# Summing the decay once per token pair in a fused RWKV6 and Hyena kernel, with one exponential, pre-multiplied k and r, chunks turned in twos, and a new order of work

## The chip, the cores and the metric

One core of one Trainium2 chip runs the program. Its engines are PE (matmul), DVE (vector), ACT (scalar), POOL (general purpose) and SP, whose queue here only issues DMA. Data that matmuls produce lies in PSUM, eight banks of 512 fp32 per partition; all other data lies in SBUF. The metric is the device time of one launch in microseconds (us). The kernel before takes 170.6 us, the median of three runs (170.54 to 171.2).

## The reference

```python
for t in range(S):                                   # S = 768, B, H, D = 4, 8, 48
    y[:, :, t] = einsum('bhd,bhde->bhe', r_t, state + outer(u * k_t, v_t))
    state = w_t[..., None] * state + outer(k_t, v_t)  # w_t in 0.8 to 0.95
x = y.transpose(0, 2, 1, 3).reshape(B, S, 384)
x1, x2, x3 = split(x @ w_proj)                        # three times 384 columns
x2 = irfft(rfft(x2, axis=1) * rfft(filter_fft, axis=0))
out = (x1 * x2 * x3) @ w_out
```

The first half is a linear recurrence over 768 steps with a decay per channel; the second is a projection, a long convolution by Fourier transforms, two gates and a projection back. All of it is fp32 outside; matmul operands are bf16 inside.

## The kernel before

**Pairs.** The recurrence runs in 12 pairs (gi, three for each of the four batches), each of two chunks of 128 steps. On a partition lie two neighbouring tokens, the even one (j = 0) and the odd one (j = 1), so a tile of k, r, v or w has 128 partitions and 8 heads x 2 x 48 elements. For each pair `lw`, `lk`, `lr` and `lv` load 384 KB each through SP's queue. `ws` multiplies the odd w by the even one, `ln` (L1245) takes logarithms of both planes, and `cs` (L1258, L1262) sums them over the tokens of a 64-token block by products with triangular matrices (`before`, `upto`, `ident`) into three PSUM banks, with the whole block's sum beside. ACT then takes exponentials: `ek` (L1267, of the negated sums, two banks into SBUF tile xk), `eq` (L1276, two banks in place) and `ph` (L1270). `km` multiplies k by xk (on DVE or POOL, from SBUF), `qm` (L1286) multiplies r by the exponentials in PSUM (DVE). `tk` and `tq` turn the products on PE and `ck`, `cq` copy them out, or, for some pairs, SP turns them by DMA (L1302).

**Within a pair.** `sc` makes scores between k and r (L1400), `mt` masks them (DVE from PSUM, or ACT's copy `ma` first and DVE from SBUF), `kv` and `su` carry the state on (L1361, L1372), `ys`, `yy` and `yi` (L1381, L1422, L1436) add up the output. `rk` is k times r, turned by `rp` and `rt` (or by DMA, L1323) for the term of u: `cp` (L1333) and `cc`, then `vc` on POOL. `xn` copies each chunk out, `yt` and `xT` (L1455, L1461) turn it for the second half.

**Second half.** When a batch's three pairs are done: `p`, `q` (gates, L1631), `xw` (side projection, L1655), `sd`, `f` (forward transform, L1486), `u`, `z` (product with the filter's spectrum), `E` (inverse, L1722), `aE`, `dE`, `yE` (folding and gating), `o` (output projection, L1793) and `so` (store). The last batch is cut finer. Before all this ACT computes the transform's tables from sines, and PE runs `warm` matmuls that only keep it busy.

**What sets the order.** A table, ORDER, lists every operation by name with the engine that does it and, for those that open PSUM banks, the bank. The program issues the operations in that order, so each engine's queue, SP's DMA queue too, has the order of its rows; waits for data and buffers are added automatically. A third word that names a DVE operation makes a POOL instruction wait for that one as well. `D` is DVE, `N` is DVE reading SBUF, `A` ACT, `G` POOL, `P` PE, `S` SP, `-` means that the operation isn't done; `warm 43 3` is 43 half-width warming matmuls.

## Time and profile before

| | |
|---|---|
| median of three runs | 170.6 us |
| the profiled execution | 171.99 us, its span 170.2 us |
| mean granted PE clock | 0.943 |
| PE, DVE, ACT, POOL busy | 140.2, 128.7, 123.3, 75.8 us |
| DMA | 32.07 MB, mean 188 GB/s |

Busy time of PE is modelled and includes the pipeline's overlap, so PE at 82% is not PE at its peak. A group's mean on the page can mix shapes; the view that keeps shapes apart doesn't. The idle time before an instruction is put down to what released it last.

### The profile page before, as it was taken

How to read it: one execution, taken by the hardware profiler on the slowest of the kernel's cores; microseconds unless marked ns; L12 is line 12 of the kernel's file. 1: busy time of each engine (PE TensorE's matmuls, PEld its weight loads, DVE VectorE, ACT ScalarE, POOL GpSimd, SP SyncE). 2: the span in 40 equal slices, each digit the busy share in tenths (PEclk: the TensorE clock that was granted, in tenths of full speed). 3: DMA queues.
4: the chain of work that ended last, by engine and by line, in shares of the span. 5: the costliest groups of instructions: out<-in, count | busy, mean ns of one | idle time of the engine just before them, and what ended most of it. 6: DMA issues, size and time to landing. Idle time of an engine off the chain costs nothing.

```text
span 170.2 us, 5650 instructions
## 1 busy us (share of the span) xinstructions
PE 140.2 (82%) x2371; PEld 90.2 (53%) x2371; DVE 128.7 (76%) x248; ACT 123.3 (72%) x196; POOL 75.8 (45%) x84
## 2 busy tenths in 40 slices
PE   7748877999889584999987789678399999999960
PEld 2326655676566352666544565455255665666520
DVE  6627989769686579399995889786248999999940
ACT  7788986876899585598997598648258586768740
POOL 7995985597459604841008940791030220002300
PEclk9978997899999999699999999999659999999997
DMA  5999979976999999989899999999912201321884
GB/s 130 312 289 293 267 181 276 273 191 89 226 221 234 260 236 252 184 162 258 223 284 174 214 191 191 193 140 174 184 27 46 49 1 62 131 88 56 323 334 119
DMA packets 77834, 32.07 MB, mean 188 GB/s; under 512 B 73841, under 2 KB 76402, under 8 KB 77810
## 3 DMA queue, kind: packets, MB, share of 16 engines
q1 hardware_dynamic: 76210, 30.55, 77.2%
q0 software_dynamic: 1600, 1.18, 4.8%
q8 instruction: 18, 0.29, 0.7%
q14 instruction: 6, 0.05, 0.1%
HBM read 22.41 MB, written 4.72 MB: 159 GB/s over the span
## 4 chain that ended last, share of the span: by engine, by line
PE 34%; DVE 13%; DMA 4%; ACT 2%; issue 2%; SPq 1%; ACTq 0%; DVEq 0%
PE banks L1631 8%; PE banks L1793 7%; PE banks L1486 7%; PE banks L1722 4%; DMA rt<-rk 4%; DVE U L1084 3%; DVE kq L1286 3%; PE banks L1655 2%; DVE mt L1084 2%; PE banks L1258 1%; DVE P L1695 1%; PE banks L1422 1%; DVE sd L1667 1%; DVE S L1372 1%; PE banks L1361 1%
## 5 line engine op out<-in xcount | busy, mean ns | idle before, releaser
L1631 PE MATMUL banks<-xT,wproj 128*128 128x384 bf16 x144 | 28.3, 326 | 2.4 <-DVE kq L1286 1.7
L1084 DVE TENSOR_TENSOR mt<-banks,causal 128x1024 bf16<-128x1024 f32 x15 | 18.1, 1218 | 6.2 <-PE banks L1400 6.2
L1088 ACT ACTIVATE x<-banks 128x768 bf16<-128x768 f32 (+1 forms) x26 | 17.9, 703 | 6.4 <-PE banks L1655 3.5
L1084 POOL TENSOR_TENSOR vc<-vb,cc 128x768 bf16<-128x768 bf16 x10 | 14.7, 1474 | 16.6 <-ACT xn L1088 10.2
L1084 POOL TENSOR_TENSOR kq<-xk,kr 128x768 bf16<-128x768 f32 x8 | 14.5, 1810 | 16.7 <-DVE U L1084 12.2
L1631 PEld LDWEIGHTS <-wproj 128*128 128x128 bf16 x144 | 13.2, 98 | 10.3 <-issue 3.0
L1084 POOL TENSOR_TENSOR g<-g,x 128x768 bf16<-128x768 bf16 (+1 forms) x4 | 5.1, 1284 | 26.0 <-DVE g L1084 17.9
L1267 ACT ACTIVATE xk<-banks 128x768 f32<-128x768 f32 x12 | 9.7, 812 | 7.7 <-PE banks L1262 7.7
L1258 PE MATMUL banks<-lg,before 128*128 128x384 bf16 x25 | 7.3, 374 | 9.5 <-DVE kq L1286 5.8
L1486 PE MATMUL banks<-sd,F 128*128 128x384 bf16 (+1 forms) x96 | 14.5, 340 | 0.0
L1655 PE MATMUL banks<-wproj,xT 128*128 128x384 bf16 x72 | 13.7, 326 | 0.1
L1793 PE MATMUL banks<-wout,y 128*128 128x384 bf16 (+1 forms) x78 | 13.3, 327 | 0.0
L1286 DVE TENSOR_TENSOR kq<-banks,kr 128x768 bf16<-128x768 f32 x12 | 11.4, 951 | 1.6 <-ACT banks L1276 1.5
L1372 DVE TENSOR_TENSOR S<-banks,phi 128x192 bf16<-128x192 f32 x20 | 7.0, 352 | 7.3 <-PE banks L1361 5.8
L1486 PEld LDWEIGHTS <-F 128*128 128x128 bf16 (+1 forms) x120 | 9.0, 112 | 6.3 <-issue 1.4
L1088 ACT ACTIVATE o<-banks 128x768 f32<-128x768 f32 (+1 forms) x12 | 9.0, 760 | 4.1 <-PE banks L1793 3.8
L1084 POOL TENSOR_TENSOR w<-w 128x384 f32<-128x384 f32 x9 | 8.9, 994 | 6.4 <-DVE kq L1084 6.4
L1084 POOL TENSOR_TENSOR rk<-kr 128x768 bf16<-128x768 f32 x6 | 10.9, 1817 | 1.4 <-DMA kr<-in_k_dram 1.4
L1400 PE MATMUL banks<-qk 48*64 48x128 bf16 x384 | 10.2, 221 | 1.3 <-DMA qk<-kq 0.8
L1084 DVE TENSOR_TENSOR U<-X,hh 128x2304 bf16<-128x2304 bf16 (+1 forms) x12 | 11.1, 952 | 0.1
L1088 ACT ACTIVATE X<-banks 128x768 bf16<-128x768 f32 x11 | 8.7, 812 | 3.3 <-PE banks L1486 2.7
L1088 ACT ACTIVATE xn<-banks 128x384 bf16<-128x384 f32 x20 | 9.0, 490 | 2.4 <-PE banks L1436 2.3
(129 smaller groups left out, 351.7 us busy)
## 6 DMA issues: line engine op xcount, KB each, us to landing
w<-in_w_dram SPq DMA_DIRECT2D x12, 384.0 KB, 5.4
v<-in_v_dram SPq DMA_DIRECT2D x12, 384.0 KB, 5.1
kr<-in_k_dram SPq DMA_DIRECT2D x12, 384.0 KB, 5.6
kr<-in_r_dram SPq DMA_DIRECT2D x12, 384.0 KB, 5.2
out_dram<-o SPq DMA_DIRECT2D x11, 384.0 KB, 2.4
U<-in_moe_filter_fft_dram SPq DMA_DIRECT2D x2, 576.0 KB, 6.5
...
```

What stands on the lines that cost most here:

```text
L1084: return eng(e).tensor_mul(o, a, b)
L1088: return nc.scalar.activation(out=o, in_=a, func=AF.Copy)
L1258: nc.tensor.matmul(p[:, z, 0:C], m, x, start=n == 0, stop=n == len(terms) - 1)
L1267: op(f"ek{gi}", [ACT], lambda e, bk: nc.scalar.activation(out=xk[sx].rearrange("p j h d -> p j (h d)"), in_=three(bk, f"cs{gi}")[:, 1:3, 0 ...
L1286: op(f"qm{gi}", [DVE], lambda e, bk: nc.vector.tensor_mul(kqq[:, 1, :, :, 0:D], three(bk, f"cs{gi}")[:, 0:2, 0:C].rearrange("p j (h d) -> ...
L1372: op(f"su{i}", [DVE], lambda e, bk, kvp=kvp, sn=sn, c=c: nc.vector.tensor_mul(stt[sn], kvp(bk), phi[sq][:, :, c:c + 1].to_broadcast([L, HP ...
L1400: nc.tensor.matmul(p[spans[c], par, i, jk, :].rearrange("p (j t) -> p j t", j=2), qkk[x, 0, jk, 2 * a + i, spans[c]], qkk[x, 1, :, 2 * a + ...
L1486: nc.tensor.matmul(p[rows], F[:, ti, c0 + rows.start:c0 + rows.stop], x[q][:, ti, :], start=(ti == 0), stop=(ti == NT - 1),)
L1631: nc.tensor.matmul(o, wproj[:, cb, col0:col0 + L], x, start=(cb == 0), stop=(cb == CB - 1))
L1655: nc.tensor.matmul(view(bk)[:, z], xT[bx][:, cb, (c0 + z) * L:(c0 + z + 1) * L], wproj[:, cb, C:2 * C], start=(cb == 0), stop=(cb == CB - 1),)
L1722: nc.tensor.matmul(o, P[:, q, m, cs], x, start=start, stop=stop)
L1793: nc.tensor.matmul(view(bk)[:, j] if full else view(bk)[spans[j]], y[cb][:, j, p0:p0 + m], wout[:, cb, :], start=(cb == 0), stop=(cb == CB ...
```

## The change

The even and odd decay are no longer summed apart. `ws` writes the product of both w to a tile of its own (wp), `ln` takes its logarithm (384 columns instead of 768), and `cs` makes two sums into two banks: `before` times it, and `upto`, now filled with -1, times it. One exponential `ex` over both banks, in place, serves k and r. To make up for the missing plane, `kw` multiplies the even k by the odd w and `rw` the odd r by the even w, after `rk` has read both; `km` and `qm` then both read PSUM, on DVE. Where the order says `ws -`, as it does for pairs 0 to 4 and 10, the product isn't made and `ln` and `cs` take both planes, with four wide products instead of two. xn holds both chunks of a pair and one `yt` and `xT` turn both, except for pair 11; xT's layout puts a chunk's blocks side by side. `u` and `z` are made in two pieces (of two and one block). Code that loads v in bf16 through POOL's queue and a second form of the inverse's copy are there too; the order uses neither. The flips of the tables (`if`) run on ACT, all six angle pieces (`ia`) on DVE. The whole order is new.

The start, on ACT: rows from the last table load on (lg is the logarithm, xk and `banks<-banks` are exponentials, phi the block's decay). Before:

```order
L1565 ACT_TABLE_LOAD
L1245 ACTIVATE lg_69<-w_61 128x8x2x48
L1245 ACTIVATE lg_70<-w_62 128x8x2x48
L1267 ACTIVATE xk_71<-banks 128x768
L1276 ACTIVATE banks<-banks 128x2x384
L1270 ACTIVATE phi_77<-banks 128x8
L1267 ACTIVATE xk_72<-banks 128x768
L1276 ACTIVATE banks<-banks 128x2x384
```

Now:

```order
L1599 ACT_TABLE_LOAD
L1271 ACTIVATE lg_71<-w_61 128x8x2x48
L1271 ACTIVATE lg_72<-w_62 128x8x2x48
L1293 ACTIVATE banks<-banks 128x2x384
L1104 ACTIVATE vb_85<-v_67 128x768
L1104 ACTIVATE cc_83<-banks 128x16
L1296 ACTIVATE phi_77<-banks 128x8
L1296 ACTIVATE phi_78<-banks 128x8
L1293 ACTIVATE banks<-banks 128x2x384
L1104 ACTIVATE qk_75<-banks 128x1024 x2
```

One exponential per pair stands where two stood, and the copy of v and the turned q and k come sooner.

POOL, early pairs (kq is the product for k, kr the tile of k and r, w the decay). Before:

```order
L1084 TENSOR_TENSOR kq_74<-xk_72,kr_65 128x16x48
L1084 TENSOR_TENSOR rk_80<-kr_65 128x768
L1084 TENSOR_TENSOR rk_79<-kr_66 128x768
L1084 TENSOR_TENSOR vc_88<-vb_85,cc_83 128x768
L1084 TENSOR_TENSOR kq_73<-xk_71,kr_66 128x16x48
L1084 TENSOR_TENSOR w_61<-w_61 128x8x48
```

Now:

```order
L1100 TENSOR_TENSOR rk_79<-kr_66 128x768
L1100 TENSOR_TENSOR kr_66<-kr_66,w_63 128x8x48 x2
L1100 TENSOR_TENSOR vc_88<-vb_85,cc_83 128x768
L1100 TENSOR_TENSOR vc_89<-vb_86,cc_84 128x768
L1100 TENSOR_TENSOR kr_64<-kr_64,w_61 128x8x48
L1105 CAST vb_87<-v_67 128x768
```

The products for k have left POOL; the halves of k and r by w, which need only loads, stand in their place.

The end, on ACT, from the last pair's xn on (x, g, ev, o, X and x_106 or x_104 are what PE made: gate, second gate, inverse, output, transform and side projection). Before:

```order
L1088 ACTIVATE xn_99<-banks 128x2x4x48
L1088 ACTIVATE x_106<-banks 128x768
L1088 ACTIVATE x_102<-banks 128x2x192 x2
L1088 ACTIVATE ev_111<-banks 128x384
L1088 ACTIVATE o_124<-banks 128x768
L1088 ACTIVATE g_103<-banks 128x4x192
L1088 ACTIVATE ev_112<-banks 128x384
```

Now:

```order
L1104 ACTIVATE xn_96<-banks 128x2x4x48 x2
L1104 ACTIVATE x_100<-banks 128x4x192
L1104 ACTIVATE x_104<-banks 128x768
L1104 ACTIVATE x_104<-banks 128x384
L1104 ACTIVATE g_101<-banks 128x2x192
L1776 ACTIVATE ev_110<-banks 128x384
L1104 ACTIVATE o_122<-banks 128x768
```

Pair 11 now runs ahead of pair 10, so the last xn is that of pair 10; behind it stand fewer of batch 2's gates, inverses and outputs than stood behind pair 11.

```diff
--- before.py
+++ after.py
-ek0 A
-km0 D
-cs1 P 4
-eq0 A
...
+ex0 A
+vb0 A
...
+qm0 D
...
+km0 D
...
@@ -1007,8 +1020,8 @@
     wl = tiles(NW, [L, H, 2, D], FP32, "w")
     kr = tiles(NR, [L, 2, H, 2, D], FP32, "kr")
     vl = tiles(NV, [L, H, 2, D], FP32, "v")
+    wp = tiles(NX, [L, H, D], FP32, "wp")
     lg = tiles(NL, [L, 2, H, DP], BF16, "lg")
-    xk = tiles(NX, [L, 2, H, D], FP32, "xk")
     kq = tiles(NK, [L, 2, 2, H, DP], BF16, "kq")
     qk = tiles(NQ, [L, 2, 2, HP, L], BF16, "qk")
     phi = tiles(NQ, [L, HP, 2], FP32, "phi")
@@ -1019,9 +1032,9 @@
     vc = tiles(NVC, [L, H, 2, D], BF16, "vc")
     mt = tiles(NM, [L, 2, 2, 2, 2, L], BF16, "mt")
     stt = tiles(NS, [L, HP, D], BF16, "S")
-    xn = tiles(NXN, [L, C], BF16, "xn")
-
-    xT = tiles(2, [L, CB, S], BF16, "xT")
+    xn = tiles(NXN, [L, 2, C], BF16, "xn")
+
+    xT = tiles(2, [L, NCH, CB, L], BF16, "xT")
     x1 = sb.tile([L, CB, 2, HALF], BF16, name="x1")
     g = tiles(2, [L, CB, 2, HALF], BF16, "g")
     sd = sb.tile([L, 2, NT, C], BF16, name="sd")
...
@@ -1235,58 +1251,66 @@
         load("w", W, w, f"w.{sw}")
         load("k", kr[sr][:, 0], k, f"k.{sr}")
         load("r", kr[sr][:, 1], r, f"r.{sr}")
...
+        def apart(bk):
             return bk[f"how ws{gi}"] == NONE
 
-        op(f"ws{gi}", [POOL, DVE, NONE], lambda e, bk: mul(e, W[:, :, 1], W[:, :, 0], W[:, :, 1]),
-           r=[f"w.{sw}"], w=[f"w.{sw}"], n=C, k="ssf")
-        op(f"ln{gi}", [ACT], lambda e, bk: nc.scalar.activation(
-            out=lgg.rearrange("p j h d -> p h j d")[:, :, :, 0:D], in_=W, func=AF.Ln),
-           r=[f"w.{sw}", "exp", "pads"], w=[f"lg.{sl}"], n=2 * C, k="s")
+        op(f"ws{gi}", [POOL, DVE, NONE], lambda e, bk: mul(e, wp[sx], W[:, :, 0], W[:, :, 1]),
+           r=[f"w.{sw}"], w=[f"wp.{sx}"], n=C, k="ssf")
+
+        def ln(e, bk):
+            if apart(bk):
+                return nc.scalar.activation(
+                    out=lgg.rearrange("p j h d -> p h j d")[:, :, :, 0:D], in_=W, func=AF.Ln)
+            return nc.scalar.activation(out=lgg[:, 0, :, 0:D], in_=wp[sx], func=AF.Ln)
+
+        op(f"ln{gi}", [ACT, ACT2], ln, r=[f"w.{sw}", f"wp.{sx}", "exp", "pads"], w=[f"lg.{sl}"], n=C, k="s", n2=2 * C)
 
         def cs(e, bk):
-            p = three(bk, f"cs{gi}")
-            le, ls = lgg[:, 0, :, 0:D], lgg[:, 1, :, 0:D]
-            if both(bk):
-                sums = (((before, le), (before, ls)), ((upto, le), (before, ls)), ((upto, le), (upto, ls)))
-            else:
-                sums = (((before, ls),), ((before, ls), (ident, le)), ((upto, ls),))
-            for z, terms in enumerate(sums):
-                for n, (m, x) in enumerate(terms):
-                    nc.tensor.matmul(p[:, z, 0:C], m, x, start=n == 0, stop=n == len(terms) - 1)
-            planes = (0, 1) if both(bk) else (1,)
+            p = two(bk, f"cs{gi}")
+            ns = (0, 1) if apart(bk) else (0,)
+            for z, m in enumerate((before, upto)):
+                for n in ns:
+                    nc.tensor.matmul(p[:, z, 0:C], m, lgg[:, n, :, 0:D], start=n == 0, stop=n == ns[-1])
             for hp in range(HP):
-                for n in planes:
-                    nc.tensor.matmul(p[:, 2, C + 2 * hp:C + 2 * hp + 2], lgg[:, n, 2 * hp:2 * hp + 2, :], chunk,
-                                     start=n == planes[0], stop=n == planes[-1])
-
-        op(f"cs{gi}", [PE], cs, r=[f"lg.{sl}", "m.before", "m.ident", "m.chunk", "pads"], new={f"cs{gi}": 3},
-           pe=[("128", C)] * 4 + [("128", 2)] * 4, pe2=[("128", C)] * 6 + [("128", 2)] * 8)
-        op(f"ek{gi}", [ACT], lambda e, bk: nc.scalar.activation(
-            out=xk[sx].rearrange("p j h d -> p j (h d)"), in_=three(bk, f"cs{gi}")[:, 1:3, 0:C], func=AF.Exp, scale=-1.0),
-           r=["exp"], w=[f"xk.{sx}", f"ek.{gi}"], uses=[f"cs{gi}"], n=2 * C, k="p")
+                for n in ns:
+                    nc.tensor.matmul(p[:, 1, C + 2 * hp:C + 2 * hp + 2], lgg[:, n, 2 * hp:2 * hp + 2, :], chunk,
+                                     start=n == 0, stop=n == ns[-1])
+
+        op(f"cs{gi}", [PE], cs, r=[f"lg.{sl}", "m.before", "m.chunk", "pads"], new={f"cs{gi}": 2},
+           pe=[("128", C)] * 2 + [("128", 2)] * 4, pe2=[("128", C)] * 4 + [("128", 2)] * 8)
+
+        def ex(e, bk):
+            p = two(bk, f"cs{gi}")[:, :, 0:C]
+            return nc.scalar.activation(out=p, in_=p, func=AF.Exp)
+
+        op(f"ex{gi}", [ACT], ex, r=["exp"], w=[f"ex.{gi}"], uses=[f"cs{gi}"], n=2 * C, k="p")
         op(f"ph{gi}", [ACT], lambda e, bk: nc.scalar.activation(
-            out=phi[sq].rearrange("p a c -> p (a c)"), in_=three(bk, f"cs{gi}")[:, 2, C:C + 2 * HP], func=AF.Exp),
+            out=phi[sq].rearrange("p a c -> p (a c)"), in_=two(bk, f"cs{gi}")[:, 1, C:C + 2 * HP], func=AF.Exp),
            r=["exp"], w=[f"phi.{sq}"], uses=[f"cs{gi}"], n=8, k="p")
 
-        def eq(e, bk):
-            p = three(bk, f"cs{gi}")[:, 0:2, 0:C]
-            return nc.scalar.activation(out=p, in_=p, func=AF.Exp)
-
-        op(f"eq{gi}", [ACT], eq, r=["exp", f"ek.{gi}"], w=[f"eq.{gi}"], uses=[f"cs{gi}"], n=2 * C, k="p")
-
-        def jhd(t):
-            return t.rearrange("p h j d -> p j h d")
-
-        op(f"km{gi}", [DVE, POOL], lambda e, bk: mul(
-            e, kqq[:, 0, :, :, 0:D], xk[sx], jhd(kr[sr][:, 0])),
-           r=[f"xk.{sx}", f"k.{sr}"], w=[f"kq.{sk}.0"], n=2 * C, k="ssf")
-        op(f"qm{gi}", [DVE], lambda e, bk: nc.vector.tensor_mul(
-            kqq[:, 1, :, :, 0:D], three(bk, f"cs{gi}")[:, 0:2, 0:C].rearrange("p j (h d) -> p j h d", h=H),
-            jhd(kr[sr][:, 1])),
-           r=[f"eq.{gi}", f"r.{sr}"], w=[f"kq.{sk}.1"], uses=[f"cs{gi}"], n=2 * C, k="ps")
+
+        op(f"rk{gi}", [POOL, DVE], lambda e, bk: mul(e, rkk, kr[sr][:, 0], kr[sr][:, 1]),
+           r=[f"k.{sr}", f"r.{sr}"], w=[f"rk.{srk}"], n=2 * C, k="ssf")
+
+
+        for m, name, j in ((0, "k", 0), (1, "r", 1)):
+            x = kr[sr][:, m, :, j]
+            op(f"{name}w{gi}", [POOL, DVE], lambda e, bk, x=x, j=j: mul(e, x, x, W[:, :, 1 - j]),
+               r=[f"w.{sw}", f"{name}.{sr}"], w=[f"{name}.{sr}"], n=C, k="ssf")
+        for m, name, t in ((0, "k", "km"), (1, "r", "qm")):
+            op(f"{t}{gi}", [DVE], lambda e, bk, m=m: nc.vector.tensor_mul(
+                kqq[:, m, :, :, 0:D], _mid(two(bk, f"cs{gi}")[:, 1 - m, 0:C].rearrange("p (h d) -> p h d", h=H), 2),
+                kr[sr][:, m].rearrange("p h j d -> p j h d")),
+               r=[f"ex.{gi}", f"{name}.{sr}"], w=[f"kq.{sk}.{m}"], uses=[f"cs{gi}"], n=2 * C, k="ps")
 
         for m, name in ((0, "k"), (1, "q")):
             t = f"t{name}{gi}"
...
@@ -1441,29 +1461,43 @@
 
         op(f"yi{gi}", [PE], yi, r=[f"vc.{svc}", "m.ident", f"yy.{gi}"], w=[f"yi.{gi}"],
            uses=[f"y{gi}.0", f"y{gi}.1"], pe=[("64", HP * D)] * 2, pe4=True)
+        sx_ = gi % NXN
         for c in (0, 1):
-            i, ci = 2 * gi + c, 2 * pi + c
-            sn_ = i % NXN
-            cols = slice(ci * L, ci * L + L)
-            op(f"xn{i}", [ACT, DVE], lambda e, bk, c=c, sn_=sn_: copy(
-                e, xn[sn_].rearrange("p (i a d) -> p a i d", a=2, d=D), yview(bk, c)),
-               r=[f"yi.{gi}"], w=[f"xn.{sn_}"], uses=[f"y{gi}.{c}"], n=C, k="p")
-
-            def yt(e, bk, i=i, sn_=sn_):
-                p = one(bk, f"yt{i}").bitcast(BF16)[:, 0:C].rearrange("p (c t) -> p c t", c=CB)
-                for n in range(CB):
-                    nc.tensor.transpose(p[:, n, :], xn[sn_][:, n * L:(n + 1) * L], ident)
-
-            op(f"yt{i}", [PE, NONE], yt, r=[f"xn.{sn_}", "m.ident"], new={f"yt{i}": 1}, pe=[("128", L)] * 3)
-
-            def turn_x(e, bk, i=i, sn_=sn_, cols=cols):
+            i = 2 * gi + c
+            op(f"xn{i}", [ACT, DVE], lambda e, bk, c=c: copy(
+                e, xn[sx_][:, c].rearrange("p (i a d) -> p a i d", a=2, d=D), yview(bk, c)),
+               r=[f"yi.{gi}"], w=[f"xn.{sx_}.{c}"], uses=[f"y{gi}.{c}"], n=C, k="p")
+
+        def turned(nm, cs_):
+            n = len(cs_)
+            ci = 2 * pi + cs_[0]
+
+            def view(bk):
+                return one(bk, "yt" + nm).bitcast(BF16)[:, 0:n * C].rearrange("p (c n t) -> p c n t", n=CB, t=L)
+
+            def yt(e, bk):
+                for z, c in enumerate(cs_):
+                    for m in range(CB):
+                        nc.tensor.transpose(view(bk)[:, z, m, :], xn[sx_][:, c, m * L:(m + 1) * L], ident)
+
+            def turn_x(e, bk):
+                o = xT[b % 2][:, ci:ci + n]
                 if e == SP:
-                    return nc.sync.dma_start_transpose(out=xT[b % 2][:, :, cols], in_=xn[sn_])
-                return copy(e, xT[b % 2][:, :, cols],
-                            one(bk, f"yt{i}").bitcast(BF16)[:, 0:C].rearrange("p (c t) -> p c t", c=CB))
-
-            op(f"xT{i}", [DVE, ACT, SP], turn_x, r=[f"xn.{sn_}"], w=[f"xT.{b % 2}.{ci}"], uses=[f"yt{i}"],
-               n=C, k="pb", q=(384, 256))
+                    return nc.sync.dma_start_transpose(
+                        out=o.rearrange("p c n t -> p (c n) t"),
+                        in_=xn[sx_][:, cs_[0]:cs_[0] + n].rearrange("p c f -> p (c f)"))
+                return copy(e, o, view(bk))
+
+            rd = [f"xn.{sx_}.{c}" for c in cs_]
+            op("yt" + nm, [PE, NONE], yt, r=rd + ["m.ident"], new={"yt" + nm: 1}, pe=[("128", L)] * (3 * n))
+            op("xT" + nm, [DVE, ACT, SP], turn_x, r=rd, w=[f"xT.{b % 2}.{ci + z}" for z in range(n)], uses=["yt" + nm],
+               n=n * C, k="pb", q=(n * C, 256))
+
+        if gi == NG - 1:
+            turned(f"{gi}.0", (0,))
+            turned(f"{gi}.1", (1,))
+        else:
+            turned(f"{gi}", (0, 1))
 
     def angles(ti):
         def fn(e, bk):
...
@@ -1839,7 +1883,8 @@
             for n in (1, 0, 2):
                 prods(n, n + 1)
         else:
-            prods(0, 3)
+            prods(0, 2)
+            prods(2, 3)
         for cb in range(CB):
             inv(cb)
         if last:
```

1646 lines of the change are left out of this document (835 added, 811 removed).

## The prediction

> **What bounds the kernel now.** I first cut the span where the program changes character: before the first pair's output is complete, while the pairs run, after the last pair, and after the last matmul. The table of stretches gives each engine's busy time (columns: stretch, its length, then PE, PEld, DVE, ACT and POOL busy with their counts, PE clock, DMA share, GB/s).
>
> ```profile
> 0.00:25.30 25.30, 18.32 (x277) 11.46 (x278) 17.30 (x60) 21.02 (x27) 21.28 (x42) 0.93 0.92 245
> 25.30:132.40 107.10, 89.81 (x1877) 59.25 (x1878) 80.60 (x122) 78.87 (x132) 50.10 (x38) 0.94 0.97 195
> 132.40:164.20 31.80, 31.80 (x220) 19.48 (x219) 30.58 (x68) 22.50 (x36) 4.40 (x4) 1.00 0.32 121
> 164.20:170.20 6.00, 0.28 (x4) 0.00 (x0) 0.18 (x1) 0.87 (x2) 0.00 (x0) 0.81 0.56 184
> ```
>
> Three different limits. The start is a chain, with no engine full. In the middle, 107.1 us long, no engine is full either: DVE has 80.6 and ACT 78.9. The tail is PE without a gap and DVE at 30.58 of 31.80: there only less work helps. The last 6.0 us are the store's way out. So I read next what PE waits for (columns: engine, line, releaser, us in total, times, longest).
>
> ```profile
> PE banks L1258 <- DVE kq L1286: 5.8, 5, 2.4
> PE banks L1258 <- ACT lg L1245: 3.4, 1, 3.4
> PE banks L1333 <- DMA rt<-rk: 3.2, 1, 3.2
> ```
>
> The decay sums (L1258) stand five times until qm of an earlier pair has given back PSUM banks; once the bonus product (L1333) waits for a transpose that went through DMA. The chain in order of time (start, us, what) shows that wait and gives the spacing of matmuls.
>
> ```profile
> 101.12 0.50 PE banks L1422 x32
> 114.82 6.89 DMA rt<-rk
> 124.59 2.04 PE banks L1486 x6
> 130.63 0.97 PE banks L1486 x6
> 132.11 0.29 PE banks L1436 x8
> 151.97 0.97 PE banks L1793 x6
> 160.30 3.88 PE banks L1793 x26
> ```
>
> Six matmuls of 384 columns take 0.97, so one takes 0.162. After the DMA wait the same six took 2.04: the wait cost 3.2 us and then about 2 us more, of which this one row shows 1.07.
>
> The price of each instruction, of which all parts below make use, is in the groups by form (count, then busy us and mean ns, then idle time before and its releaser).
>
> ```profile
> L1267 ACT ACTIVATE xk<-banks 128x768 f32<-128x768 f32 x12 | 9.7, 812 | 7.7 <-PE banks L1262 7.7
> L1276 ACT ACTIVATE banks<-banks 128x768 f32<-128x768 f32 x12 | 9.6, 797 | 0.3
> L1245 ACT ACTIVATE lg<-w 128x768 bf16<-128x768 f32 x12 | 9.9, 840 | 0.0
> L1084 POOL TENSOR_TENSOR kq<-xk,kr 128x768 bf16<-128x768 f32 x8 | 14.5, 1810 | 16.7 <-DVE U L1084 12.2 <-ACT xk L1267 4.6
> L1084 DVE TENSOR_TENSOR kq<-xk,kr 128x768 bf16<-128x768 f32 x4 | 3.8, 952 | 2.0 <-ACT xk L1267 2.0
> L1286 DVE TENSOR_TENSOR kq<-banks,kr 128x768 bf16<-128x768 f32 x12 | 11.4, 951 | 1.6 <-ACT banks L1276 1.5
> L1084 POOL TENSOR_TENSOR w<-w 128x384 f32<-128x384 f32 x9 | 8.9, 994 | 6.4 <-DVE kq L1084 6.4
> L1084 POOL TENSOR_TENSOR rk<-kr 128x768 bf16<-128x768 f32 x6 | 10.9, 1817 | 1.4 <-DMA kr<-in_k_dram 1.4
> L1084 POOL TENSOR_TENSOR vc<-vb,cc 128x768 bf16<-128x768 bf16 x10 | 14.7, 1474 | 16.6 <-ACT xn L1088 10.2 <-ACT cc L1088 3.6 <-DVE w L1084 1.5
> L1084 DVE TENSOR_TENSOR w<-w 128x384 f32<-128x384 f32 x2 | 1.1, 552 | 0.0
> L1084 DVE TENSOR_TENSOR mt<-banks,causal 128x1024 bf16<-128x1024 f32 x15 | 18.1, 1218 | 6.2 <-PE banks L1400 6.2
> L1084 DVE TENSOR_TENSOR mt<-mt,causal 128x1024 bf16<-128x1024 bf16 x9 | 6.1, 686 | 1.1 <-ACT mt L1088 1.1
> L1088 ACT ACTIVATE mt<-banks 128x1024 bf16<-128x1024 f32 x9 | 9.2, 1025 | 1.4 <-PE banks L1400 1.2
> L1088 ACT ACTIVATE xn<-banks 128x384 bf16<-128x384 f32 x20 | 9.0, 490 | 2.4 <-PE banks L1436 2.3
> ```
>
> **The start.** Rows of the timeline, and the page's row of bytes (40 slices of 4.255 us).
>
> ```profile
> GB/s 130 312 289 293 267 181 276 273 191 89 226 221 234 260 236 252 184 162 258 223 284 174 214 191 191 193 140 174 184 27 46 49 1 62 131 88 56 323 334 119
> 9.94 1.58 ACT L1245 ACTIVATE lg<-w 128x768 bf16<-128x768 f32 x2
> 10.83 0.71 PE L1258 MATMUL banks<-lg,before 128*128 128x384 bf16 x2 [3.43 <-ACT lg L1245]
> 12.30 0.81 ACT L1267 ACTIVATE xk<-banks 128x768 f32<-128x768 f32 x1 [0.79 <-PE banks L1262]
> 13.15 0.80 ACT L1276 ACTIVATE banks<-banks 128x768 f32<-128x768 f32 x1
> 20.42 1.21 DVE L1084 TENSOR_TENSOR mt<-banks,causal 128x1024 bf16<-128x1024 f32 x1
> 23.14 1.22 DVE L1084 TENSOR_TENSOR mt<-banks,causal 128x1024 bf16<-128x1024 f32 x1 [0.64 <-PE banks L1400]
> 24.92 0.36 PE L1436 MATMUL banks<-vc,ident 64*64 64x192 bf16 x8
> ```
>
> Today the first logarithm starts at 9.94 and yi0 ends at 25.28. The changed order keeps three table loads and four sines ahead of the logarithm on ACT, so I leave 9.9. Behind it, per step at the durations above: ln0 0.8, cs0 1.0 (its warming matmuls stand right ahead of it, while today PE idles 3.43), one exponential 0.8 instead of two, qm and km on DVE 1.9, transposes and two copies of 1024 columns on ACT (1.0 each, as its mask copies) until 16.1, scores, two masks of 1.2 one behind the other, until 19. That reaches yi0 at about 20. The loads set a floor: ahead of yy0 on PE's queue stand cs2, rp2, ki2 and kv2, and w of pair 2 is the tenth load of 0.393 MB; 3.93 MB have come by 15.6 us at the rates of the row, then ln2, cs2 and the others need some 4 us. On POOL rk, kw, rw and vc (1.8, 1.0, 1.0, 1.5) follow the ninth load and end near 19.5. I take 20.5, a gain of **4.8**; bounds 20 and 24, the latter if the loads land as late as today's masks do.
>
> **The pairs.** ACT loses the 12 xk exponentials (9.7) and half of six logarithms (6 x 0.35 = 2.1; a logarithm of 384 columns lies between the 0.49 of ACT's xn and 0.84, and I take 0.49); four mask copies go as well (4.1). It takes over the table flips, some copies and spectrum scalings, some 9. Net **-6.6**. DVE: km 4 to 12 (+7.6, at the price of qm, which reads the same two banks), masks 15 to 19 from PSUM and 9 to 4 from SBUF (+1.5), kw and rw six at 0.55 (+3.3); away go flips, vc, two rk and several copies. Net **-0.9**. POOL loses eight km (14.5) and four products of w, and gains 18 of kw and rw (17.9), two rk and two vc: +4 or so; it had 50.1 of 107.1. None of these three is full in the middle, so their totals cost nothing by themselves. On the way from the sums to k and q, today 0.81 + 1.81 to k (exponential, POOL) and 0.81 + 0.80 + 0.95 to q; then 0.80 + 0.95 to the first and 0.95 more to the second. The way to q shortens by 0.8, that to k stays, and the banks are held 2.7 us as before, but two rather than three.
>
> PE: cs needs 36 products of 384 columns instead of 50, -2.3; 22 more transposes, 20 more two-column products and a wider inverse add 2.0 by the same counting, so PE's work hardly falls: -0.3. What matters is where it lies. I counted each matmul between the first and the last yi in the order and gave it its kind's spacing (0.162 for 384 columns, 0.50/32, 0.29/8 and so on): 77.8 us today, 83.1 then, since 4.6 come from the tail and 1.1 from the start. Today 77.8 took 107.1, a rate of 0.73. At that rate 83.1 take 114.4: **+7.3**. But 5.8 + 3.2 of the idle time hang on things the change touches, the three banks and the late rt. I give it 3.6 of these 9.0, not all, since km now reads the banks behind qm: **110.8, +3.7**. Bounds: 104 (all that is pulled in fits into idle time and both waits go) and 114.4.
>
> **The tail.** In the order, after the last yi, stand 193 matmul slots of 0.162 today (a 64-row or 192-column one counts half): 31.4, and the chain took 31.8 from 132.40 to 164.2. In the changed order there are 165: 12 gate, 12 output and four inverse slots fewer. That is 26.8, with the same 0.4 of loss 27.2. DVE must follow: it has 56 instructions after its last mask, where today it has 64 and needs all of its 30.58; by the same kinds' steps they come to some 25, so PE stays the limit. The xT of the last pair goes by DMA in one piece of two chunks; ahead of its first reader PE has 5.2 us of other work, against 0.9 for the two xn and the landing. A turn of six blocks lies between these two (three blocks of xT, eight of qk; median us to landing):
>
> ```profile
> xT<-xn SPq DMA_TRANSPOSE x16, 3.3
> qk<-kq SPq DMA_TRANSPOSE x13, 4.6
> ```
>
> I take 27.3: **-4.5**; bounds 27 and 30, the latter if that turn lands 3 us late.
>
> **The sum.** 20.5 + 110.8 + 27.3 + 6.0 = 164.6 of span, against 170.2. The profiled execution took 171.99 us, 1.8 above its span, while the median of the three runs is 170.6, 0.4 above it; I carry the 0.4: **165.0 us**.
>
> **Rivals.** (1) *The middle keeps its rate.* For it: km moves to DVE and the banks wait is on DVE; loads keep DMA at 0.97 through the middle. Then 114.4: 168.2 of span, 168.6 us, still faster. (2) *Transposes by DMA land late, and PE stands for them more than once.* rt of the last four pairs still goes by DMA, behind other transposes and loads on SP's queue, and cp9, cp10 and cp11 stand in PE's queue ahead of everything else.
>
> ```profile
> DMA to landing us min/median/max: 2.8/4.2/6.9
> ```
>
> With two such stalls instead of one, at 5.2 us each, on the kept rate: 168.2 + 5.2 = 173.4, 173.8 us, **slower**. It decides from about 3 us of further standing. Against it: rt10 and rt11 are issued together behind the xT of pair 8, and I count 12 us of PE work between that pair's yi and cp10. The clock that follows such a wait is part of the price. The Trainium skill, "TensorE: Matmul & The Clock Gate", section "What's actually happening", states that PE drops to half clock after an idle window of about 3.4 us; the row of 2.04 after a wait of 3.16 is near to that. (3) *POOL in DVE's way.* The change puts 18 new two-input products on POOL, early in each pair, when DVE does rk, rw and copies in SBUF. The trace has such delays: the same flip took between 311 and 972 ns, the long one while POOL was at rk.
>
> ```profile
> L1094 DVE TENSOR_SCALAR mx<-mi,sgn x2: 311/642/972, 18.1 to 25.3; 128x384 bf16<-128x384 bf16 x2
> ```
>
> If half of the 18 cost a DVE instruction 0.66 on the chain, that is 5.9: 170.5 of span, 170.9 us, no change. The Trainium skill, "SBUF — State Buffer", section "SBUF: two separate sides", says that such an instruction and POOL's lock each other out for a whole instruction; the row agrees. Against it: POOL's total hardly grows, the flips leave DVE, and the order ties four of the 18 behind a DVE instruction.
>
> **Chances.** Forecast 0.60, rival 1 0.18, rival 2 0.13, rival 3 0.09. The range: the forecast's own runs from 160 (start and middle near their good bounds) to 168; rival 1 belongs in, rival 3 nearly all, and rival 2 up to its first half stall, 171.5. With 0.5%, about what this kernel's runs can tell: faster (under 169.7) 0.78, the same 0.09, slower 0.13.
>
> **What would show it.** Right: yi0 ends between 20 and 22; the last yi near 131; PE after it about 27 us without a gap, DVE just under; the wait of the sums for DVE kq under 4 us; ACT total near 117, DVE near 128. Wrong: yi0 after 23 (the loads), the last yi after 135 (the middle at its old rate or below), PE standing for rt, qk or xT by over 3 us, or a gap in the tail ahead of the last xw.

## The result, and the profile after

The changed kernel takes 160.8 us, the median of four runs (158.9 to 161.4), against 170.9 us of the kernel before beside it (170.5 to 173.4): a ratio of 0.938, with a 95% interval from 0.927 to 0.949. The forecast was 165.0, so the sign is right and the gain, 10.1 us for 5.6, nearly twice as large as forecast. Executions of one kernel differ by up to some per cent, and the ratios leave out the longest of them. The profiled execution took 161.4 us; its span is 159.7, where the prediction summed up 164.6.

The same cut as before, at the end of the first yi, of the last yi and of the last matmul (stretch, its length, then PE, PEld, DVE, ACT and POOL busy with counts, PE clock, DMA share, GB/s), changed kernel:

```profile
0.00:22.95 22.95, 19.37 (x267) 11.23 (x268) 18.74 (x58) 18.58 (x25) 14.74 (x38) 0.93 0.96 255
22.95:126.41 103.46, 92.20 (x1952) 63.21 (x1953) 85.18 (x134) 77.32 (x136) 59.18 (x49) 0.95 1.00 198
126.41:153.71 27.30, 27.30 (x190) 16.61 (x189) 25.99 (x62) 20.18 (x33) 3.65 (x4) 1.00 0.39 141
153.71:159.70 5.99, 0.00 (x0) 0.00 (x0) 0.00 (x0) 0.74 (x2) 0.00 (x0) 0.94 0.58 200
```

| stretch | before | predicted | after |
|---|---|---|---|
| start, to the end of yi0 | 25.3 | 20.5 | 22.95 |
| middle, to the end of the last yi | 107.1 | 110.8 | 103.5 |
| tail, to the last matmul | 31.8 | 27.3 | 27.3 |
| drain | 6.0 | 6.0 | 6.0 |

The tail and the drain came out as worked out. The start gave half of what was expected, and the middle, which was to grow by 3.7 us because work was pulled into it, shrank by 3.6: PE's busy time there grew by 2.4 (89.81 to 92.20) and its idle time fell by 6.0 (17.3 to 11.3). So two questions go to the chip: what kept the start, and what the middle was paid with.

The page's line of busy times (share of the span, instructions) fits the counting: ACT 116.8 where about 117 was expected, DVE 129.9 for 128.

```profile
PE 138.9 (87%) x2405; PEld 91.1 (57%) x2405; DVE 129.9 (81%) x252; ACT 116.8 (73%) x194; POOL 77.6 (49%) x91
```

What PE waits for in the middle (engine, line, releaser, us in total, times, longest), changed kernel:

```profile
PE banks L1401 <- issue: 4.3, 1, 4.3
PE banks L1665 <- ACT x L1104: 2.0, 1, 2.0
PE banks L1520 <- ACT X L1104: 0.8, 3, 0.3
PE banks L1665 <- DMA wproj<-in_moe_w_proj_dram: 0.7, 1, 0.7
```

and, from the same view of the kernel before, rows that the prediction did not show:

```profile
PE banks L1258 <- DVE kq L1286: 5.4, 4, 2.4
...
PE banks L1381 <- issue: 1.9, 1, 1.9
PE banks L1631 <- DVE kq L1286: 1.7, 2, 1.2
PE banks L1381 <- DVE kq L1286: 0.9, 1, 0.9
...
PE banks L1400 <- DMA qk<-kq: 0.8, 1, 0.8
```

Before, PE stood 8.0 us in the middle for DVE's k and q products (5.4 + 1.7 + 0.9) and 4.0 us for transposes by DMA (3.2 + 0.8). None of these rows is left; of the waits of the sums (now L1282) one of 0.4, for ACT's mask copy, remains. In their place stands one of 4.30 us "for issue", which means: for nothing that the profile shows. It lies in the middle of an operation, as the timeline of PE shows (start, us, line, tiles, count, and in brackets the idle time ahead):

```profile
34.98 0.28 PE L1456 MATMUL banks<-vc,ident 64*64 64x192 bf16 x4
35.81 0.28 PE L1456 MATMUL banks<-vc,ident 64*64 64x192 bf16 x4 [0.56 <-issue]
...
41.26 0.34 PE L1381 MATMUL banks<-vb,kq 64*64 64x48 bf16 x11 [0.32 <-issue]
...
45.80 0.38 PE L1401 MATMUL banks<-S,qk 48*64 48x48 bf16 x24
50.48 0.31 PE L1401 MATMUL banks<-S,qk 48*64 48x48 bf16 x8 [4.30 <-issue]
```

24 of the 32 products of ys8 and ys9 run, then PE stands, then the other eight follow, though all of them need the same two things. The three breaks stand behind 607, 734 and 862 matmuls, each with its weight load, that is 254 and 256 instructions apart. The chain of waits passes through the same 10 us by another thing, a load of wproj that took 11.01 us, and the gate behind it ran its six matmuls in 2.10 instead of 0.97:

```profile
39.50 1.37 POOL vc L1100
40.88 11.01 DMA wproj<-in_moe_w_proj_dram
51.88 0.05 issue
51.93 2.10 PE banks L1665 x6
```

### The profile page after: what moved, and what is told of

Same layout as the page of the kernel before. It is cut to its first block, busy times and chain, and to the rows that moved or that the text cites. A ratio compares the mean times of both kernels' runs of the same rounds, so it can differ in the third digit from the quotient of the medians.

```text
span 159.7 us, 5717 instructions
## 1 busy us (share of the span) xinstructions
PE 138.9 (87%) x2405; PEld 91.1 (57%) x2405; DVE 129.9 (81%) x252; ACT 116.8 (73%) x194; POOL 77.6 (49%) x91
## 4 chain that ended last, share of the span: by engine, by line
PE 49%; ACT 14%; DMA 13%; DVE 6%; issue 4%; POOL 4%; ACTq 0%; POOLq 0%; DVEq 0%
PE banks L1665 11%; PE banks L1520 7%; DMA wproj<-in_moe_w_proj_dram 7%; PE banks L1837 6%; PE banks L1689 6%; PE banks L1756 5%; DMA kr<-in_k_dram 4%; DVE kq L1310 3%; PE banks L1442 3%; ACT X L1104 2%; DMA out_dram<-o 2%; PE banks L1282 2%; PE banks L1420 2%; POOL vc L1100 2%; PE banks L1381 2%
## 5 line engine op out<-in xcount | busy, mean ns | idle before, releaser
L1100 DVE TENSOR_TENSOR mt<-banks,causal 128x1024 bf16<-128x1024 f32 x19 | 23.1, 1220 | 7.6 <-PE banks L1420 6.5
L1310 DVE TENSOR_TENSOR kq<-banks,kr 128x768 bf16<-128x768 f32 x24 | 22.2, 951 | 5.3 <-ACT banks L1293 2.6
L1100 POOL TENSOR_TENSOR vc<-vb,cc 128x768 bf16<-128x768 bf16 x12 | 17.6, 1471 | 17.3 <-DVE y L1100 8.1
L1100 POOL TENSOR_TENSOR kr<-kr,w 128x384 f32<-128x384 f32 x18 | 17.9, 999 | 7.5 <-DVE rk L1100 3.1
L1104 ACT ACTIVATE g<-banks 128x768 bf16<-128x768 f32 (+1 forms) x14 | 9.1, 657 | 9.2 <-PE banks L1665 9.1
L1520 PE MATMUL banks<-sd,F 128*64 128x384 bf16 (+1 forms) x96 | 14.2, 334 | 0.6 <-ACT X L1104 0.6
L1100 DVE TENSOR_TENSOR U<-X,hh 128x768 bf16<-128x768 bf16 (+1 forms) x18 | 11.9, 683 | 0.2
L1293 ACT ACTIVATE banks<-banks 128x768 f32<-128x768 f32 x12 | 9.6, 804 | 2.3 <-PE banks L1285 2.3
L1126 PE MATMUL banks<-wt 128*128 128x512 bf16 (+1 forms) x31 | 9.2, 450 | 1.1 <-DVE scl L1189 1.1
L1401 PE MATMUL banks<-S,qk 48*64 48x48 bf16 x320 | 5.8, 190 | 4.9 <-issue 4.3
L1837 PEld LDWEIGHTS <-y 128*128 128x128 bf16 (+1 forms) x78 | 6.9, 99 | 4.8 <-issue 0.3
```

The lines of the kernel that those rows point to most:

```text
L1100: return eng(e).tensor_mul(o, a, b)
L1104: return nc.scalar.activation(out=o, in_=a, func=AF.Copy)
L1126: nc.tensor.matmul(banks[:, at, lo:hi], wt[:, 0:L], x, start=True, stop=True)
L1293: return nc.scalar.activation(out=p, in_=p, func=AF.Exp)
L1310: op(f"{t}{gi}", [DVE], lambda e, bk, m=m: nc.vector.tensor_mul(kqq[:, m, :, :, 0:D], _mid(two(bk, f"cs{gi}")[:, 1 - m, 0:C].rearrange("p ...
L1401: nc.tensor.matmul(yview(bk, c)[spans[j], par, hp, :], qkk[x, 1, j, hp, spans[c]], stt[so][x, hp, :], start=hp == 0, stop=False,)
```

## The experiments

The kernel before ran beside each set, with medians of 172.9 to 173.6 us, more spread than in the first set; ratios are given where its runs allow one. The changed kernel was run again in the second set (e5), and e4, a single run that differs from it by 38 idle instructions, stands for it in the first.

**The start: the small exponential ahead (e3).** In the order, ph (the block's decay, eight columns) moves up in all twelve pairs; this is pair 0.

```diff
 ex0 A
+ph0 A
 ...
 qm0 D
 ...
 km0 D
 cc0 A
-ph0 A
```

> The changed kernel with one thing moved: the small exponential ph (the block's decay, 0.18 us) of each pair stands right behind ex, ahead of qm and km, where it stood behind km for nine pairs and waited there for DVE's reading of the bank (3.8 us in all, with the next work of ACT behind it; 1.1 us of it at 14.6 us, ahead of the second pair's exponential). Theory 'ACT's queue was held': these waits go, the first pair's output (yi0) ends 1 us earlier, at about 21.9, and the time falls by 1 to 2.5 us against the changed kernel, to 158 to 160. Rival: km and qm now wait 0.2 us for ph in each pair and nothing is won: 160.5 to 162, yi0 at 23.

It took 157.1 us (156.9 to 160.3), a ratio of 0.907 [0.899, 0.915], and yi0 ended at 21.69. The theory holds, and the gain is larger than it said. The timelines of ACT and PE show the place. Changed kernel:

```profile
14.64 0.24 ACT L1296 ACTIVATE phi<-banks 128x8 f32<-128x8 f32 x2 [1.12 <-DVE kq L1310]
14.91 0.80 ACT L1293 ACTIVATE banks<-banks 128x768 f32<-128x768 f32 x1
15.62 1.94 ACT L1104 ACTIVATE qk<-banks 128x1024 bf16<-128x1024 bf16 x2
...
17.07 0.24 PE L1387 MATMUL banks<-S,ident 128*128 128x192 bf16 x1 [1.49 <-DVE S L1392]
...
18.96 0.78 PE L1282 MATMUL banks<-lg,before 128*128 128x384 bf16 x2
```

With ph ahead:

```profile
14.22 0.81 ACT L1293 ACTIVATE banks<-banks 128x768 f32<-128x768 f32 x1
...
16.60 0.24 PE L1387 MATMUL banks<-S,ident 128*128 128x192 bf16 x1 [0.39 <-DVE S L1392]
...
18.49 0.50 PE L1282 MATMUL banks<-lg,before 128*128 128x384 bf16 x2
```

ph and km only read the same bank, but the program makes the later reader wait for the earlier. ph stood behind km in the program, so ACT waited 1.12 us for DVE, with the second pair's exponential behind it in ACT's queue; DVE's next product was late by that, the state's update after it, and PE stood 1.49 us. After this gap two products of 384 columns take 0.78 instead of 0.50. The stretches of 2 us show why: the granted clock (third number from the end). Changed kernel:

```profile
17.00:19.00 2.00, 1.79 (x74) 1.48 (x74) 2.00 (x5) 1.36 (x3) 2.00 (x3) 1.00 1.06 289
19.00:21.00 2.00, 2.00 (x21) 1.35 (x19) 2.00 (x2) 1.20 (x3) 2.00 (x2) 0.51 0.69 179
21.00:23.00 2.00, 2.00 (x63) 1.51 (x60) 1.38 (x4) 2.00 (x4) 0.63 (x1) 0.64 0.99 240
```

With ph ahead:

```profile
19.00:21.00 2.00, 1.61 (x48) 1.33 (x48) 2.00 (x3) 1.39 (x3) 2.00 (x3) 1.00 0.90 223
21.00:23.00 2.00, 2.00 (x59) 1.63 (x51) 1.96 (x4) 2.00 (x4) 1.29 (x1) 1.00 0.87 220
```

The start was held by a gap that nobody would count, and by the clock that PE lost through it. Further on, ACT's waits of ph for DVE (3.8 us in all) are gone too, while DVE now waits four times for ph, 1.2 us in all. The stand of 4.30 us for "issue" was 0.22 in this run, and the middle took 100.2. How the gain divides is not settled: against the changed kernel's profile yi0 ends 1.3 us sooner and the middle is 3.3 shorter, against e4's it is 3.1 and 0.6, and whether the shorter stand is owed to the move is not shown.

**The stand for "issue": is it the instruction stream? (e4)** One warming matmul at the start makes room for 20 tiny ones, 38 instructions more on PE in all.

```diff
-warm 22 2
+warm 20 2
+warm 20 2 2     # twenty products of two columns
```

> The changed kernel with 38 more instructions on PE's stream at the start (20 products of two columns in place of one warming product), nothing else. In the changed kernel PE stood 4.30 us in the middle of an operation, 24 products into ys8 and ys9 with nothing that they wait for; breaks of 0.32 and 0.56 us, also inside an operation, stand 256 and 510 instructions ahead of it. Theory 'the instruction stream': a break comes at every 256th instruction whose code lands late, so it moves with the count: the stand is then found 38 instructions earlier in the program, behind about 5 products of ys8, at about the same time (46 us) and 2 to 6 us long. Rival 'something the work waits for': the break stays ahead of the 25th product. Time within 1.5 us of the changed kernel by both.

160.55 us, and the break moved to where the count put it: 27 of the 32 products now stand behind it, five ahead.

```profile
50.27 0.40 PE L1406 MATMUL banks<-S,qk 48*64 48x48 bf16 x27 [3.06 <-issue]
```

So the stand does not belong to the work; its place goes by the count of PE's instructions. The kernel before agrees: its stand of 1.93 us comes behind 991 matmuls, and with matmuls put in (e12, below) one of 1.68 comes behind 991 again, now inside a warming matmul. The Trainium skill, "Runtime: NRT & Kernel Launch", section "Instruction fetch mechanics", says that an engine's instructions are fetched by DMA in blocks of 256, at a cost that is mostly hidden. The spacing of 254 and 256 agrees; hidden it was not here, with 4.30 and 3.06 us.

The trace holds the fetch itself: the view of the DMA queues has one named "instruction" (queue, packets, MB, share of the 16 engines' time). The changed kernel's line for the whole run, and for 48.0 to 49.3 us:

```profile
q8 instruction: 19, 0.31, 0.8%
...
q8 instruction: 1, 0.02, 5.4%
```

These 19 blocks are PE's: it has 4810 matmuls and weight loads, and no other engine has more than 252 instructions that keep it busy. Between 41.3 and 48.0 us this queue moved nothing; then it moved one block, by the trace's packets from 48.06 to 49.18, and PE, standing since 46.18, went on at 50.48. In all fourteen profiles together PE stands 29 times for "issue", and each time it goes on 1.3 to 1.7 us after a block of this queue has landed. So PE stood for its code. The block itself moves in about 1 us; what is late is its start.

**What is in its way? (e5, e6, e7)** e5 is the changed kernel once more.

> The changed kernel once more, to stand beside the next three in the same set: 159 to 162 us, a ratio near 0.935 to the kernel before.

161.6 us (160.1 to 163.3), with a stand of 3.63 us at the same instruction. e6 puts the filter's loads later, e7 the last two pieces of wproj earlier.

```diff
-filt1 S
...
-filt0 S
...
 lv6 S
...
 lw8 S
+filt1 S
+filt0 S
```

> The changed kernel with the two loads of the filter (1.15 MB, first read at 53.8 us) moved behind the loads of r for pair 7 and of w for pairs 7 and 8 on SP's queue. In the changed kernel they are issued at 38.4 us, just ahead of the last two pieces of wproj (issued 40.9, landed 51.9, 11.0 us after issue). Theory 'backlog': with 1.15 MB less in front, wproj lands within 8 us, PE's stand of 4.30 us on its instruction stream at 50.5 shrinks under 1.5, and the time falls by 3 to 6 us against the changed kernel. Rival: the DMA engines are full up to 60 us anyway, and what is moved comes in the way of the pairs' loads or the filter's first reader: within 1 us of the changed kernel, or slower.

```diff
 wproj1 G
+wproj2 G
+wproj0 G
...
-wproj2 G
...
-wproj0 G
```

> The changed kernel with the last two pieces of wproj issued on POOL's queue right behind the first (at about 33 us instead of 40.9), the filter left where it is. Theory 'backlog': wproj lands ahead of its reader (0.7 us of wait gone), but the bytes in flight up to 46 us are the same, so PE's stand on its instruction stream stays between 2 and 5 us; 159 to 161 us. Rival 'wproj is what PE stands for': the 4.30 us go with it; 155 to 157 us. A loss is possible too: the pairs' loads behind it land up to 3 us later.

e6: 166.0 us (162.4 to 167.6). Its shortest run lies within the range of e5, so that it is slower is likely but not shown; a gain of 3 to 6 us, as expected of the backlog, is ruled out. In the profile (of a run of 166.2 us) wproj landed in 7.2 us and the stand shrank, but to 1.98 only, by the timeline of PE:

```profile
50.66 0.25 PE L1401 MATMUL banks<-S,qk 48*64 48x48 bf16 x8 [1.98 <-issue]
```

and DVE then stood for the filter, by the waits of the same run:

```profile
DVE P L1609 <- DMA U<-in_moe_filter_fft_dram: 6.5, 1, 6.5
```

e7: 157.4 us (157.3 to 157.7), 4 us faster than e5 by the medians, and every run of it is shorter than every run of e5. In PE's timeline no stand for "issue" behind the start is longer than 0.72 us, and by the table of stretches the middle took 97.9:

```profile
24.14:122.00 97.86, 89.67 (x1952) 61.53 (x1953) 84.62 (x134) 76.89 (x135) 59.31 (x49) 1.00 1.04 206
```

My theory of the bytes in flight said that e7's stand would stay at 2 to 5 us; it fell. In e7 the same block of code moved at 44.0 to 45.1 us, ahead of PE, which passed the place at 47.5. What lets the block through early is not shown. wproj's own bytes were not in its way: of their 0.59 MB the changed kernel had moved 0.03 by 48.0 us (wproj is issued at 40.9), while SP's queue moved 1.38 between 41.3 and 48.0. Nor does the stand come whenever wproj's loads span that moment: in e3 they do (issued at 41.6, landed by 51.3), and it was 0.22.

**What the exponential was worth (e2).** A second exponential of the two banks, into a tile that nobody reads, ahead of each pair's ex.

```diff
+ek0 A
 ex0 A
...
+        op(f"ek{gi}", [ACT], lambda e, bk: nc.scalar.activation(
+            out=xk.rearrange("p (j c) -> p j c", j=2), in_=two(bk, f"cs{gi}")[:, :, 0:C], func=AF.Exp, scale=-1.0),
+           r=["exp"], w=["xk"], uses=[f"cs{gi}"], n=2 * C, k="p")
```

> The changed kernel with the exponential that was removed put back: ahead of each pair's exponential ACT takes another one of the same two banks, of the negated sums, into an SBUF tile that nobody reads; 12 x 0.8 = 9.7 us more on ACT. Theory 'chain': the exponential is on the way from the sums to k and q, and where the chain passes that way (about four pairs) it costs its 0.8: 2 to 4 us more than the changed kernel, 163 to 165. Rival 'ACT has room' (116.8 of 159.7 busy): under 1 us more, 160 to 162. Rival 'ACT's total': 8 to 10 us more, 169 to 171.

165.9 us (165.4 to 166.5), a ratio of 0.957 [0.948, 0.967]. That is 5.4 us more than e4, a single run, in the same set; by the ratios to the kernel before (0.957 and 0.938) it is 3.3 more. So the price is some 3 to 5 us: by the first more than "chain" said, by the second within it, and in both short of "ACT's total". Against e4 all of it is in the middle, by the stretches of e2:

```profile
24.88:131.15 106.27, 92.65 (x1952) 63.13 (x1953) 84.93 (x136) 84.33 (x146) 59.19 (x49) 0.97 0.98 188
```

and of e4:

```profile
24.79:125.59 100.80, 91.16 (x1952) 62.63 (x1953) 84.49 (x134) 77.14 (x136) 59.12 (x49) 0.97 0.99 201
```

The waits of DVE's products for ACT double. With the second exponential:

```profile
DVE kq L1327 <- ACT banks L1310: 7.5, 7, 2.1
```

e4:

```profile
DVE kq L1315 <- ACT banks L1298: 3.6, 3, 2.3
```

ACT has 77 of 101 us in the middle and is nobody's bound, and yet 8 us more of busy time on it (124.5 for 116.5) cost 3 to 5: in a queue that is served in order, what stands behind is late by 0.8 in each pair, and seven times a product waited for it. Not all of the 5.5 us between the two middles need be this: PE's stands for "issue" add up to 4.9 us in e2's and 3.5 in e4's.

**What work moved into the middle costs (e12).** The kernel before, with two and a half warming matmuls behind ten of its yi: 25 x 0.162 x 512/384 = 5.4 us of work for PE.

```diff
 yi0 P
+warm 5 6
 ...
 yi2 P
+warm 5 6
```

> The kernel before, with 5.4 us of matmuls more in the middle, that nobody reads: behind ten of the first eleven yi stand two and a half warming matmuls of 512 columns (0.216 each). It tests the step by which work moved into the middle was priced at the middle's rate (77.8 us of work in 107.1, 0.73). By that step it costs 7.4 us: 177 to 179 on a base of 170.6. Rival 'waits don't grow with work': PE stands for others 17 us of the middle anyway, the work goes into those gaps or at most beside them: 0 to 5.4 us, 170.5 to 176.

176.2 us (174.7 to 178.2), a ratio of 1.027 [1.014, 1.040] to the kernel before. Its middle:

```profile
24.72:135.99 111.27, 95.09 (x1907) 60.76 (x1908) 81.24 (x122) 79.56 (x132) 50.03 (x38) 0.95 0.93 189
```

That is 4.2 us more than the 107.1 of before, for 5.4 us of work: 0.77 us per us. Idle time takes up a quarter of it and does not grow with it. The rule of the middle's rate, 1.38 us per us or 7.4 here, does not hold, though by little: the ratio's interval is 2.5 to 6.9 us.

**What the pre-multiplication costs (e11).** kw and rw are left out; half of k and r then lack a factor.

```diff
-rw0 D
+rw0 -
...
-kw0 G
+kw0 -
```

> The changed kernel without the 24 products that multiply the even k and the odd r by w (18 on POOL, 6 on DVE; the result then lacks one decay factor in half of k and r). It measures what the pre-multiplication costs. Theory of the prediction, that totals off the chain cost nothing: 1 to 2 us faster than the changed kernel, mostly the six on DVE (3.3 us busy) and those of the start; 159 to 160. Rival 'POOL's chain rk, kw, rw stands ahead of k and q': 4 us faster or more, 157 or less.

159.6 us (159.4 to 160.0), a ratio of 0.934 [0.924, 0.943]: about 1 us below the changed kernel, inside its spread. So leaving out 21 us of products on POOL and DVE gains next to nothing. That this is their price is not shown, since the profile has a new delay in their place: DVE's product of the two w (wp, 0.55 us in the changed kernel) took 3.59 us beside POOL's vc and rk, and PE then waited 2.92 us for the state's update behind it.

```profile
42.47 3.59 DVE L1100 TENSOR_TENSOR wp<-w 128x384 f32<-128x384 f32 x1
```

**Chunks turned one by one (e10).**

```diff
-yt4 - 0
+yt4.0 - 0
+yt4.1 - 0
...
-xT4 S
+xT4.0 S
+xT4.1 S
```

> The changed kernel with the turning of chunks in twos undone: the same transposes into the same bank, but two copies of 384 columns in place of one of 768 for five pairs, and two DMA transposes of three blocks in place of one of six for six pairs. Theory: on the engines it is 5 x 0.2 us, and six more turns on SP's queue, whose landing nobody waits for: within 1 us of the changed kernel, 160 to 162. Rival: the turns were on the way and their number counts: 2 us or more slower, 163 to 165.

163.7 us (161.4 to 165.5), a ratio of 0.948 [0.932, 0.965]. The interval overlaps that of the changed kernel; the profiled spans are equal (159.7), with a stand of 2.07 us for "issue" here and 4.30 there. What the trace shows is 2.0 us of waiting for rt and 0.9 for xT by DMA, in two places each, behind six more turns on SP's queue. Turning in twos is worth 0 to 3 us; this run can't say more.

**The arithmetic without the order (e1, e8).** The old order of work with the new arithmetic dropped in (pair 2 of e1, against the order of the kernel before).

```diff
+rk2 G
+kw2 G
+rw2 G
 ck0 A
-ek2 A
+ex2 A
...
-eq2 A
...
 qm2 D
+km2 D
 ph2 A
-rk2 G
...
-km2 G
```

> The changed arithmetic (product of both w, one exponential over two banks, k and r pre-multiplied, km on DVE from PSUM) put into the old order of work: each pair's kw and rw stand ahead of its sums (18 of the 24 on POOL, 6 on DVE), the chunks are turned one by one, the products with the spectrum are made in one piece, pair 11 stays behind pair 10. Theory 'the order did it': the banks are free sooner, so the sums' wait for DVE (5.4 us in the middle before) halves, the bonus product's wait for the late DMA transpose (3.2 us) stays, the tail stays at 31.8; 166 to 170 us, that is less than half of the gain of 9.8. Theory 'the arithmetic did it': the shorter way from the sums to k and q and the freed exponentials carry the gain; 160 to 164 us, the sums' wait for DVE under 1.5 us.

> The changed arithmetic in the old order of work a second time, without the two things that the first attempt put in its way: the small exponential ph stands right behind ex (two of them right behind the state's update that frees its tile), not behind km, where ACT stood 41.1 us for it, and rk, kw and rw stand as early as their loads and tiles allow, not right ahead of the sums. Theory 'the order has to fit': 172 to 185 us, no faster than the kernel before, with DVE's km and qm waiting for POOL's kw and rw. Rival 'only ph was in the way': 160 to 168 us.

e1: 197.4 us (196.6 to 200.6), a ratio of 1.139 [1.127, 1.150]. e8: 205.0 us (two runs). Both theories on each missed. In e1 the small exponential stood for DVE, and DVE for POOL's kw and rw:

```profile
ACT phi L1307 <- DVE kq L1321: 41.1, 11, 8.2
POOL kr L1111 <- DVE rk L1111: 26.2, 4, 9.8
...
DVE kq L1321 <- POOL kr L1111: 14.8, 4, 5.9
```

In e8 ph no longer waits, but the early rk, kw and rw stand for loads ahead of the angle tables on DVE, and the chain still passes through POOL:

```profile
107.42 0.88 DVE rk L1111
108.37 3.46 POOL kr L1111 x2
...
115.31 3.65 DMA kr<-in_k_dram
119.10 1.80 POOL rk L1111
```

k and r are now changed in place, so a load, rk (1.8 us on POOL), kw and rw (1.0 each) follow one another ahead of km and qm, and the next load into the tile waits for those. The old order gives this row no lead. Both ran at a granted clock of 0.83, for 0.94 in the kernel before. How much of the 24 and 31 us over the kernel before beside them is the arithmetic's and how much my placing is not settled by two attempts. They show that the arithmetic does not pay in these two placings, not that it brings nothing by itself, so how the gain divides between arithmetic and order stays open.

**Three mends together (e9).** ph ahead, wproj early, and a fifth output tile, because the last output copy of the changed kernel stands for a store:

```profile
155.12 0.49 ACT L1104 ACTIVATE o<-banks 128x384 f32<-128x384 f32 x1 [1.16 <-DMA out_dram<-o]
```

```diff
-NXN, NO = 2, 4
+NXN, NO = 2, 5
...
-            s = slot[0] % NO
+            s = {0: 4, 1: 2, 2: 3, 3: 0}[k_] if last else slot[0] % NO
```

> Three mends of the changed kernel together: ph right behind ex (alone 157.1 us), the last two pieces of wproj issued right behind the first (alone 157.4), and a fifth output tile with the last four copies given the tiles that were stored first, since in the changed kernel the last copy stands 1.16 us until a store has left its tile. If the three waits are apart, their gains add up, 4 + 4 + 1.2 of 161: 151 to 153 us. Rival: the first two take away the same stand (PE's 4.30 us on its instruction stream, which both made small), so that only one of them counts: 155 to 157.

155.8 us (153.7 to 156.2), a ratio of 0.904 [0.886, 0.923]: it beats both kernels, and is 1.3 and 1.6 us below ph and wproj alone, which ran in other sets; by the ratios it can't be told from ph alone (0.907). The gains do not add up, as the rival said: either one takes away the same stand. The output tile did what it should for the copy, and it was worth nothing: the drain is 5.77 us instead of 5.99.

```profile
148.63:154.40 5.77, 0.00 (x0) 0.00 (x0) 0.00 (x0) 0.62 (x2) 0.00 (x0) 0.87 0.56 187
```

## Why the prediction was right, and where it was not

**The start** (20.5 forecast, 22.95 measured, 23.2 to 24.8 in e4, e5 and e10). The step that failed is "transposes and two copies of 1024 columns on ACT until 16.1 ... scores, two masks ... until 19". The copies ended at 17.6 and the masks at 21.1: the step had no ph in ACT's queue, which waits for km (1.12 us), and none of it had a gap on PE, after which the sums of pair 2, rp2, ki2 and kv2 run at half the clock ahead of yy0. With ph ahead it is 21.69 (e3) and 21.13 (e9), inside the 20 to 22 that I called right. The price of the clock was named for the DMA wait only; it belonged here too.

**The middle** (110.8 forecast, 103.5 measured, 100.8 in e4). By the tables of stretches, with the 5.3 us of pulled-in work as busy time, the forecast leaves PE 15.7 us of idle time; measured were 2.4 more of busy time and 11.3 of idle time, and the two differences, 2.9 and 4.4, make up the 7.3. Two terms were mis-sized, in opposite sense to the start. First, "At that rate 83.1 take 114.4: +7.3": the 5.3 us of pulled-in work cost 0.77 each by e12, that is 4.1, so 3.2 less. Second, "None of these three is full in the middle, so their totals cost nothing by themselves": e2 shows that twelve exponentials on ACT, put back, cost 3 to 5, with 3.9 us more of waits of the products for k and q. I had part of that in "I give it 3.6 of these 9.0"; all of the 9.0 went, and 3.4 more of waits for kq and qk that I had not listed. Against these stands what I did not foresee: the stand at the code break, 4.30 us where the kernel before has 1.9. 110.8 - 3.2 - (9.0 - 3.6) + 2.4 is 104.6, near the 103.5; this sum is arithmetic on separate runs, not a measurement of its own, and it is not complete: the 3.4 would take it to 101.2, and new waits of PE, 2.0 for ACT and 0.7 for wproj, back to 103.9.

**The tail** was right in the term and in the number: 165 slots, 27.3 forecast, 27.30 measured, PE without a gap, DVE at 25.99 where some 25 were counted. The drain is as it was.

**The last 0.4.** Each run of the changed kernel lies 1.7 above its span, as the kernel before's profiled run did (1.8); the 0.4 compared a median with another run's span. With 1.8 the forecast would have been 166.4. By span the forecast was 4.9 too high, by time 4.2.

**The rivals.** (1) The middle kept its rate: refuted by e12 as a rule and by the 103.5 as a number. (2) Transposes by DMA landing late: no wait of PE for rt, qk or xT is in the list of the changed kernel. Among its variants e10 has the most (2.0 us for rt, 0.9 for xT), where six more turns were on the queue, and e3, e7, e9 and e11 have 0.2 to 0.7; so the mechanism exists, and the 3 us at which it was to decide were not reached. (3) POOL in DVE's way: one mask of 0.69 took 1.85 while POOL was at vc, and among the products of that line no other form spread by more than 0.1, so it cost some 1.2 us; DVE's other lines were not searched. That such a delay can cost more e11 shows, where one took 3.0 us and PE stood 2.92 behind it, with kw and rw not even there. The two rows of the changed kernel, POOL's and DVE's, from its timeline:

```profile
39.46 1.48 POOL L1100 TENSOR_TENSOR vc<-vb,cc 128x768 bf16<-128x768 bf16 x1
39.63 1.85 DVE L1100 TENSOR_TENSOR mt<-mt,causal 128x1024 bf16<-128x1024 bf16 x1
```

The time was right within its range because the start's miss (+2.5) took back a third of the middle's (-7.3). That was luck: the range began at 160, 0.8 below what was measured, and with the start as forecast the time would have lain below it.
